# Attention and FFN on one core: TensorE work moved from two tile shapes to 64x32 tiles on two row lanes

## The chip, the cores and the metric

The kernel runs on one core of one Trainium2 chip. The metric is the device time of one execution in microseconds; of several runs the median is given.

## What is computed

`x` has 2048 rows of 640. It is normalised row by row, and two branches read the result: attention with 32 heads of 20 that share one key and one value head, and an FFN with 1728 inner features.

```
xn = layernorm(x)                                  # 2048 x 640
q  = xn @ wq  -> 32 heads of 2048 x 20;  k = xn @ wk;  v = xn @ wv     # one k, one v
p  = softmax(q k^T / sqrt(20));  o = p v           # 32 x 2048 x 2048 scores
out = x + o @ wo + silu(xn @ w1) @ w2
```

Everything is bf16 at the edges, and sums are fp32 in PSUM.

## The kernel before

**Blocks.** The scores are cut into 2048 blocks. A block is one head, 128 keys and 512 queries (one of four chunks of queries); it fills one PSUM bank with keys on the partitions. Four heads make a group. A head sits on 32 partitions (a slot) of `qT` and `kT`: 20 rows of data, two rows for an offset, the rest zero.

**Scores (L1133).** A visit takes up to four blocks, each of another head, on the four row tiles of 32 rows by 128 columns. All blocks of a visit run side by side, one pass of 512 columns.

**Exponentials.** A block's exponentials come from ScalarE (L1156, an exp over one, two or three banks that lie next to each other, into `E`) or from VectorE (L1173). VectorE takes the score, offset by 16045 through the two extra rows, as the bits of a bf16 number; two copies with the phase shifted (L1201 on VectorE or L1207 on GpSimd, three blocks at once) are averaged with it, which gives such a block three PV products in place of one. Only these blocks carry the offset: `kT` is held twice, without it for ScalarE and with it for VectorE.

**PV (L1047).** For a group of four heads, values times exponentials are summed in bank 7 (`UBANK`), each head on its own column tile of 128 rows by 32 columns. A set is one product for each of the four heads. When a group is complete, `end_group` copies the sums out (L1251), a DMA transposes them, and they are divided by their sum.

**Projections (L533, `cols`).** Jobs for q, for the FFN's inner layer (`h`) and for the output (`F`) run as steps of four matmuls, also 128x32, with 512 or 320 columns, and sum in one of the other seven banks.

**Order.** `Sched` is a planner that runs while the program is built: it keeps a clock for each engine, and a price and readiness time for each operation; its result is a fixed order on each queue with semaphores. TensorE's own order is written out by hand from the 64th block on: `ORDER` holds a letter for each step, P for a PV set, J for a projection step, and other letters for score visits, with how many blocks a visit has and how many of them go to VectorE in `VISITS`. `follow` reads it. Ahead of it the start-up (loads, normalisation, keys, values, the first queries) is planned without a list, and behind it `tail` ends the last groups.

**Keys (L1889 to L1906).** `k_job` projects keys; VectorE copies them from PSUM (L1901) and GpSimd makes the second copy with the offset (L1903).

Of the kernel before, what the change touches and what calls it, by code (L numbers as in the profile page):

```python
# [39 lines left out]
OFF_LO = 45.0  # L40
PH = ((0, 1.0), (43, 0.8046875), (86, 0.625))
# [37 lines left out]
RANK = "UofFhqG"  # L79
YIELD = 0.65  # L80
VISITS = {"a": (3, 0), "b": (3, 1), "c": (3, 2), "e": (4, 1), "f": (4, 2), "g": (2, 0), "h": (2, 1), "k": (1, 0), "m": (1, 1), "d": (4, 3)}
ORDER = (
    "BBPPPHMPPGePPPFPPPbJJJJJeMJJJJJPbPPPBfPPMbPBPPPEPPPckPPPHBJJJBJJPBmPPbhhPPBPJGPJJFJPJBGJJJPJJFPPPPgP"
    "PHHPPhgJPPcJKHPhGPPCkJJgHPPPJHbPPPbPPbJJBJPCJJBPPPAPPJbJPJhGJPPdPJgPPPbPPbJJbPJBJJBPJGJJfPJJPbPPBPPP"
    "FPPBPPBJJJJJfGPPPJJJCJJPBgPJPPJBJJJBJJJJJbPPbPPPFPPbPPbPPfJJJJJBGPPJPJJFPJPJPbhJJJJJBGPPPPPfPPbJJJBJ"
    "JbPJJJbPJJBPJJbPJJbJJJbPJJbPPFPPPBPPfPPBJJJJJbPPbJJJJBPPJbJJBJJPPbPPfPPBPPPEPJJJBJJBJPPbJJPbJJJbJPJb"
    "JJJJbPJJbPPFPPBPPBPPEPJPJJbJJJJPbJJBPPJJbPJJJbPPfPPbPPbPPbPPEJJJJBPJPBJPBJJJJbJPJbJJJbJJJJbPPePPPPFP"
    "PBPPFPPaPJJJBJJJJPbJJJBJJJJbPPePPPHhPPPFPPBJJJBJJbJJPJBJJJaPPJJJbJJJJJbPPbPPfPPPBPePPPPFPPPBPPPEJPJJ"
    "JJHbJJJPJBJJJBJPJbPPFPPbPPEPJJJbJJPBJPBJPJJJFgPPPPPPbPPfJJJJJbhJJJJJPePPPPPBcJJJJJBHJJJJJPePPPPBPPfP"
    "PBJJbJJJbPJJPBJJJbPPbJJJJJBJJhJJJePPPPbPPfPPBJJJJJbbPPPPPPFPPBJJJbJJbPPBJJbJJJbPPPPePPBJPJJfJJPJJJgb"  # L90
    "JPPPJPfPPBPPBJJBJJJPbPPPBPPBJJJJBJJJJBJJJbJJJJbJJJJbPFPPPPFPbPPPBPPfPPaPJJBJJPJEPPPBPPPFPPbJJJJJBJJb"
    "JJJPBJPJBJPJbPJJBJJJBPPEPPPPFPPPbPJJbJJJBPJJbJPPbJPJbPJJBJJJbPJJbPJJBPPePPPbPPBJPJPfJPgJJPfPPBPPBJJJ"
    "JBJJJBJJJJBPPBJPJBPJJBJJPBJJPbPPEPPbJJPJJJJEJPJPJJhBPPJBPJJJBJJJBPJJbPPfPPBPPPePPPPFPPbPJJBJJbPJbPPP"
    "fPPBJJPJBJJBJJJJJJeJJJPJJbJJJbPPePPPPPDgPPPbPPPBJJPBJPJBJJJBJPPBJPbPJJbPJJBPJJbJJJJbPPFPPBPPEPJJJJJb"
    "JJJBPJJbJPJbJJJBPPPBJJJJbPPePPPPfPPbPPPbPPfPPbJJJJJbBPPPJJJBJJPJbJJJJPbbPPPJJBJJJPbPbPJJJbJJBPPPPfPP"
    "PbJJBJJJPePPPPBPBJPPJfJJPJPbHJJJJJPfJJJJJPeJJJJJPBbPPPPJbPJBJJbPJbPPBPPfPPbJJJbJJbJJPJbJPJbJJPJbJJPB"
    "PPFPPBJJJJJbbPPPJJPBJJJBPPPbPPPBPPePJJJbJJBPPBPPfPPPbJJJBJJJJbJJJbPJJBPJPbPJBJPPbJJJJbPPFPPAPPPFPPJJ"
    "JBJJPBJJJbJJJJbJJJbJJJJBPPePPBJJPJeJJPPBPPbPPPfPPbPPPFPPbPPBPPEPJJJJJBJJJJBPJJJBJJJBJJJJbPPfPPBPPPeP"
    "JJJJJBJJPBPPbJJPBJJPBPJJJBJJJBPJJbPPfPPPBPPEPPPPFPPbJJJBJPJbPbPPPFPPBJJJJbJJPJJJJfgJJJJJJJJbPJPBPPfP"
    "PBPPBPPFPPbJPJJBPPBJPJBJJJbJPJBPJJBPJJbJJPbPPbJJPJBPPEPJPJPBJJJBPJJBPJJBJPJbPJJBJPJbJPJBJPJbPPfPPBPP"  # L100
    "PePJJJJJBJJJbJJJJbPJJBJJJJBJPbPPPFPPbPPBPPePPJJBJJJPePJJJJhJPePPPPbPPPFPPBJJJJJBbPPPJJJcJJPBgPJJJJJM"
    "ePPPPPPBPfPPJJBJPbPJJbJJhJJJPeJJJJJhBJPJJJJBPPPPfPPBJJJJJbBPPPPPPfPPbJJJbJJbPJPJbJPCJJPgBPJJPJJJbPPP"
    "bPPBJPJBJJJBJPJBJPJBJJJJBJJJBJJPBPPJbPPfPPBPPPePJJJJJbJJJbJJJJbJJJBJJJJbPPfPPAPPPfPPPPFPPBPJJJBJJbJJ"
    "JJJaJJPJJJbJJJJbPPEPPPPfPPPPfPPBPPbPPfPPBJJJJBJJPBJJJbJJPBJJPbPPBJJJJbJPJBPPEPJPJJJBJJJBPPbPJJBJPPBJ"
    "JJBJJJJbJJPBPPFPPBPPaPPPFPPPbPPFPPBJJJJBJPJBJJPbJPPJbJbPPJJJeJJJJJPbPPfPPbPPPFPPAPPBJJJJJJFJJJJGJJJE"
    "JJJJJJbPPFPPbPPFPPBPPEPPbJJJPJJEPPPJJBJJJbPJJBJPPbPPbJPJbJJbJJPbPPFPPbPPbPPBFPBPPBPPbPPFPPBPPAPPBfBP"
    "PBPEPPPFPbPbPPEPPBPPPkbPJJJJJJBJJPbPPEPPA"
# [44 lines left out]
class Op:  # L152
    __slots__ = ("eng", "dur", "fn", "deps", "prio", "seq", "end", "avail", "idx", "inc", "inc_no", "sem",
                 "on_sched", "name", "dma", "mode", "start", "mm", "work", "then", "lock", "rep", "tile", "kt", "w", "x", "na", "at")
# [24 lines left out]


LAT = {"pe": 0.215, "act": 0.27, "dve": 0.14, "pool": 0.19, "sp": 0.0}
# [4 lines left out]
class Sched:  # L186
    def __init__(self, nc, stack):
# [11 lines left out]
        self.held = {}  # L199
        self.lock_end = {"dve": 0.0, "pool": 0.0}  # L200
# [45 lines left out]
    def ready(self, op, extra=0.0):  # L246
        r = op.at
        for d in op.deps:
            if d.avail is None:
                return INF  # L250
            if d.eng == op.eng and not d.dma:
                if op.eng == "pe" or op.eng == "sp":
                    a = d.end
                else:
                    a = d.avail - OWN[op.eng]
# [14 lines left out]

    def commit(self, op, start):
        e = op.eng
        op.start = start
# [8 lines left out]
        op.idx = len(self.order[e])  # L282
# [56 lines left out]
    def emit(self):  # L339
# [3 lines left out]
        every = sorted((op for e in self.engs for op in self.order[e]), key=lambda op: (op.start, op.end, op.idx))  # L343
        for op in every:
            e = op.eng
            mine = seen[e]
            need = {}
            for d in op.deps:
                if d.rep is not None:
                    d = d.rep  # L350
                if not d.dma and d.eng == e and e in ("pe", "sp"):
# [17 lines left out]
        sems = {e: self.sem("done_" + e) for e in self.engs}  # L369
        for e in self.engs:  # L370
            n = 0
            for op in self.order[e]:
                if op.inc and not op.dma:
                    n += 1
                    op.inc_no = n
        out = {e: [] for e in self.engs}
        for e in self.engs:
            for op, w in per[e]:
                def fn(eng, op=op, w=w, e=e):
# [8 lines left out]
                    elif op.inc:  # L388
                        ins.then_inc(sems[e], 1)
# [32 lines left out]
class Job:  # L422
    def __init__(self, name, mms, reads, consume, gate=None, min_step=-1, banks=None, on_start=None, width=0, hold=None, use=None, n=1, mode="M"):
# [14 lines left out]
        self.last = False  # L438
        self.spot = 0


class Builder:
# [17 lines left out]
    def alloc(self):  # L460
# [41 lines left out]
        self.offk = sb([P, 1], F32)  # L502
# [28 lines left out]
    def cols(self, pe, b, n, w, x, start, stop):  # L531
        for j in range(0, w.shape[-1], SLOT):
            ins = pe.matmul(self.bk(b, 0, n, j, j + SLOT), w[:, j:j + SLOT], x, start=start, stop=stop,  # L533
                            tile_position=(0, j), skip_group_check=True)
# [5 lines left out]
    def steps_init(self):  # L540
# [23 lines left out]
        self.pv_started = False  # L564
        self.tq = [[[] for _ in range(4)] for _ in range(self.NG)]
# [101 lines left out]
    def s_reads(self, bs, dv):  # L667
        k = []
        for i, (g, kt, j) in enumerate(bs):
            c, h = g // 8, 4 * (g % 8) + j  # L670
            k += [("kT1" if i in dv else "kT", kt // 2), ("kT", kt // 2), ("qb", c % 2, h)] + self.qkeys(c, h)
# [63 lines left out]
    def step(self, now):  # L735
# [3 lines left out]
        if 0 <= self.at < len(ORDER):  # L739
            return self.follow(ORDER[self.at], now)  # L740
        if self.b_next >= NB:
            return self.tail(now)
# [89 lines left out]
    def follow(self, tok, now):  # L832
        nxt = INF
        if tok == "P":
            n, _, nxt = self.pv_ready(now)
            if n:
                self.do_pv(now, T_PE + self.switch("PV"))
                self.at += 1
                self.stall = 0
                return True  # L840
            if self.debt:
                self.debt -= 1
                self.at += 1
                self.stall = 0
                return self.step(now)
            for d in self.sc.deps_of((), [("UB",)]):
                if d.avail is not None and d.avail > now:
                    nxt = min(nxt, d.avail)
        elif tok == "J":
            job = self.cur_job  # L850
            r = now
            if job is not None and job.step_reads and job.last and self.reads_ready(job.step_reads[0]) > now + 1e-9:
                self.at += 1
                return self.step(now)
            if job is None:
                self.more_jobs()
                r = self.job_ready(self.misc[0]) if self.misc else INF
            if r <= now + 1e-9:
                if job is None:
                    job = self.misc.popleft()  # L860
                    job.bank = self.bank_for_job(job)[1]
                    self.cur_job = job
                    if job.hold is not None:
                        self.heldb[job.hold] = job.bank
                self.do_mm(job, now, job.mms[0][0] + self.switch(job.mode))
                self.at += 1
                self.stall = 0
                return True
            nxt = r
        else:  # L870
            n, nd = VISITS[tok.lower()]
            bt = self.bank_times()
            r = max(self.reads_ready(self.s_reads(self.blocks(n), range(n) if nd else ())), bt[n - 1][0])
            if not self.room(n - nd, nd):
                full, some, _ = self.pv_ready(now)
                if full or some and self.stall > 8:
                    self.do_pv(now, T_PE + self.switch("PV"))
                    self.debt += 1
                    return True
# [1122 lines left out]
```

## Time and profile before

| | |
|---|---|
| three runs | 680.76, 682.35 and 683.6 us; median 682.35 |
| the profiled execution, first to last instruction | 681.4 us |
| granted TensorE clock in it, mean | 0.997 |
| matmuls | 9690 |
| instructions on VectorE, ScalarE, GpSimd | 1103, 765, 455 |

The profiled execution has no time of its own beside its span; the span lies 0.95 us under the median of the runs and inside their range. Views of the trace name engines PE (TensorE's matmuls), PEld (its weight loads), DVE (VectorE), ACT (ScalarE) and POOL (GpSimd). A row of the groups holds the line, the engine, the operation, its tiles and shapes and the count, then behind bars the busy time, the mean of one in ns, and the idle time ahead of them with what ended it. A row of the timeline begins with its start and length, with neighbours of one kind merged. The end of a matmul is modelled in the trace, its start is not.

### The profile page before, as it was taken

Reading aid. Unit: us, or ns where it says so; the run is one execution under the profiler, and the core shown is the slowest. Engines: PE = TensorE matmul, PEld = TensorE weight load, DVE = VectorE, ACT = ScalarE, POOL = GpSimd, SP = SyncE. Lnnn points to the kernel's source line nnn. Section 1 sums busy time; section 2 is a strip of 40 time slices with the busy share of each in tenths; the row PEclk is TensorE's granted clock in tenths of the full one; section 3 lists DMA queues with packets and bytes.
Section 4 is the critical chain, followed back from the end, with each engine's and each line's share of the span. In section 5 each row is a group of like instructions: output and inputs, shape, how many; then the busy total and the mean of one; then the engine's idle time right before and its main releaser. Section 6 shows DMA issues by size and latency. Waiting matters only on the chain.

```text
span 681.4 us, 22653 instructions
## 1 busy us (share of the span) xinstructions
PE 669.8 (98%) x9690; PEld 230.8 (34%) x9690; DVE 623.7 (92%) x1103; ACT 661.3 (97%) x765; POOL 563.9 (83%) x455
## 2 busy tenths in 40 slices
PE   9899999999999999999999999999999999999997
PEld 4333323333333333333333333333333333333323
DVE  7879999999899999999999999999989999999996
ACT  6989999999999999999999999999999999999995
POOL 5559888888888998887888899788899898878873
PEclk9989999999999999999999999999999999999999
DMA  7457301000103000011012000001011100000002
GB/s 207 88 203 234 116 18 14 6 14 18 17 17 55 11 9 19 23 23 37 19 29 61 10 17 23 24 17 32 15 29 48 29 10 12 11 19 20 20 17 64
DMA packets 53241, 28.18 MB, mean 41 GB/s; under 512 B 39094, under 2 KB 52502, under 8 KB 53142
## 3 DMA queue, kind: packets, MB, share of 16 engines
q1 hardware_dynamic: 52854, 26.40, 15.2%
q8 instruction: 78, 1.28, 0.8%
q10 hardware_dynamic: 288, 0.33, 0.1%
q14 instruction: 21, 0.17, 0.1%
HBM read 11.44 MB, written 2.62 MB: 21 GB/s over the span
## 4 chain that ended last, share of the span: by engine, by line
PE 81%; ACT 10%; DVE 7%; DMA 1%; issue 1%; ACTq 0%
PE psall L1047 28%; PE psall L1133 25%; PE psall L533 25%; ACT sbt L1156 10%; DVE sbt L1173 3%; PE psall L967 1%; DMA sbt<-sbt 1%; DVE sbt L1722 1%; DVE sbt L1201 1%; DVE sbt L1403 1%; PE psall L1893 1%; PE psall L954 0%; DVE sbt L1885 0%; DVE sbt L1251 0%; PE psall L1297 0%
## 5 line engine op out<-in xcount | busy, mean ns | idle before, releaser
L1156 ACT ACTIVATE sbt<-psall 128x1024 bf16<-128x1024 f32 (+2 forms) x680 | 626.5, 1056 | 5.5 <-PE psall L1133 4.9
L1207 POOL TENSOR_TENSOR sbt<-sbt 128x768 int32<-128x768 int32 (+2 forms) x378 | 526.2, 1418 | 87.0 <-DVE sbt L1201 74.6
L1173 DVE TENSOR_SCALAR sbt<-psall 128x512 int16<-128x512 f32 x711 | 466.1, 684 | 41.2 <-PE psall L1133 32.7
L1047 PE MATMUL psall<-sbt 128*32 128x512 bf16 x3470 | 281.3, 385 | 0.3 <-DVE sbt L1901 0.2
L1133 PE MATMUL psall<-sbt 32*128 32x512 bf16 x2048 | 251.4, 384 | 2.4 <-ACT sbt L1156 1.0
L533 PE MATMUL psall<-sbt 128*32 128x320 bf16 (+1 forms) x3863 | 235.1, 331 | 0.3 <-DVE sbt L1173 0.3
L1133 PEld LDWEIGHTS psall<-sbt 32*128 32x128 bf16 x2048 | 66.4, 91 | 235.9 <-issue 87.7
L533 PEld LDWEIGHTS psall<-sbt 128*32 128x32 bf16 x3863 | 87.0, 95 | 86.5 <-issue 43.0
L1047 PEld LDWEIGHTS psall<-sbt 128*32 128x32 bf16 x3470 | 70.8, 95 | 102.4 <-issue 71.0
L1201 DVE TENSOR_SCALAR sbt<-sbt 128x1536 int16<-128x1536 int16 (+1 forms) x114 | 65.9, 583 | 0.6
L1403 DVE SCALAR_TENSOR_TENSOR sbt<-sbt,psall 128x512 bf16<-128x512 bf16 (+1 forms) x56 | 37.9, 677 | 0.1
L1395 ACT ACTIVATE sbt<-psall 128x512 bf16<-128x512 f32 x54 | 33.9, 627 | 0.9 <-PE psall L533 0.4
L1239 POOL TENSOR_TENSOR sbt<-sbt 128x320 bf16<-128x320 bf16 x31 | 22.6, 729 | 5.4 <-DVE sbt L1201 5.4
L1251 DVE CAST sbt<-psall 128x512 bf16<-128x512 f32 x31 | 21.2, 684 | 1.2 <-PE psall L1047 1.0
L967 PE MATMUL psall<-sbt 128*128 128x512 bf16 (+3 forms) x66 | 18.0, 403 | 1.6 <-DVE sbt L1656 1.2
L1501 DVE SCALAR_TENSOR_TENSOR sbt<-psall,sbt 128x320 bf16<-128x320 f32 x28 | 13.4, 487 | 1.3 <-PE psall L533 0.9
L1352 DVE TENSOR_SCALAR sbt<-psall 128x512 bf16<-128x512 f32 (+1 forms) x19 | 13.0, 684 | 0.9 <-PE psall L533 0.7
L1722 DVE BATCH_NORM_STATS2 sbt<-sbt 128x6 f32<-128x320 bf16 x24 | 10.4, 468 | 2.6 <-DMA sbt<-in_A_x_dram 2.6
L1903 POOL TENSOR_SCALAR sbt<-sbt 128x256 bf16<-128x256 bf16 x8 | 3.8, 479 | 9.8 <-DVE sbt L1752 5.7
L1748 POOL TENSOR_SCALAR sbt<-sbt 128x640 bf16<-128x640 bf16 x7 | 6.1, 877 | 5.0 <-DVE sbt L1790 3.7
L967 PEld LDWEIGHTS psall<-sbt 128*128 128x128 bf16 x66 | 6.1, 105 | 10.3 <-issue 4.0
L1893 PE MATMUL psall<-sbt 128*128 128x256 bf16 x40 | 5.9, 274 | 3.3 <-DVE sbt L1924 1.4
(80 smaller groups left out, 90.1 us busy)
## 6 DMA issues: line engine op xcount, KB each, us to landing
sbt<-in_A_x_dram SPq DMA_DIRECT2D x31, 160.0 KB, 3.4
out_dram<-sbt SPq DMA_DIRECT2D x15, 160.0 KB, 1.8
sbt<-in_B_w_dram SPq DMA_DIRECT2D x5, 432.0 KB, 5.4
sbt<-sbt SPq DMA_DIRECT2D x105, 20.0 KB
sbt<-in_B_w_dram SPq DMA_DIRECT2D x13, 160.0 KB, 3.0
sbt<-sbt SPq DMA_DIRECT2D x1, 1024.0 KB, 6.5
sbt<-sbt SPq DMA_TRANSPOSE x58, 2.5
sbt<-in_A_wo_dram SPq DMA_DIRECT2D x5, 160.0 KB, 2.8
```

What stands on the lines that cost most here:

```text
L533: ins = pe.matmul(self.bk(b, 0, n, j, j + SLOT), w[:, j:j + SLOT], x, start=start, stop=stop, tile_position=(0, j), skip_group_check=True)
L967: return pe.matmul(self.bk(b, 0, n), self.zero[:, 0:P], self.zero[:, 0:n], start=True, stop=True)
L1047: ins = pe.matmul(self.bk(UBANK, 0, QW, r, r + SLOT), self.v[:, it.w, it.kt, :], it.x(), start=f, stop=False, tile_position=(0, r), skip_g ...
L1133: ins = pe.matmul(self.bk(bank[i]), self.kT[r:r + SLOT, 1 if i in dv else 0, kt * P:(kt + 1) * P], self.qT[r:r + SLOT, g % 8, (g // 8) % 2 ...
L1156: return a.activation(self.E[:, (b0 + lo) * QW:(b0 + lo + m) * QW], self.ps[:, b * BANK:(b + m) * BANK], AF.Exp, scale=ACT_SCALE)
L1173: return v.tensor_scalar(self.Z[:, zs, zp * QW:(zp + 1) * QW], self.bk(bb), 0.0, ZMAX, ALU.max, ALU.min)
L1201: sc.new("dve", td, lambda v, k=k: v.tensor_scalar(self.Y[:, zs, k, 0:w], self.Z[:, zs, 0:w], float(PH[k + 1][0]), None, ALU.add), zk, yk, ...
L1207: sc.new("pool", tp, lambda v, k=k, cb=cb: v.tensor_tensor(self.Y[:, zs, k, 0:w].bitcast(I32), self.Z[:, zs, 0:w].bitcast(I32), cb, ALU.ad ...
L1239: op = sc.new(eng, 0.75 if eng == "pool" else t_dve_ps(16 * DH), lambda v: v.tensor_tensor(dst, ut[:, :, :, 0:DH], rb, ALU.mult), [key, (" ...
L1251: ev = sc.new("dve", t_dve_ps(QW), lambda v: v.tensor_copy(self.U[:, up, :], self.bk(UBANK)), [("UB",)], [("U", up)], prio=U_PRIO, name=f" ...
L1395: sc.new("act", t_act(QW), lambda a: a.activation(t, src, AF.Tanh, scale=0.5), [("B", b)], [("tb", tp)], prio=X_PRIO, name=f"th{c}_{fk}")
L1403: sc.new("dve", t_dve_ps(QW), lambda v, r0=r0, r1=r1, ht=ht: v.scalar_tensor_tensor(out=ht[r0:r1, :], in0=t[r0:r1, :], scalar=1.0, in1=src ...
```

## The change

From the 64th block on no TensorE work uses the two old shapes. The array is cut into two row lanes, rows 0 to 63 and 64 to 127, with four column tiles of 32 each; every step is four matmuls on one lane.

- A score block is one lane's step. It takes 64 rows, that is two heads' slots, and `kT` now holds two copies that each keep only the even or only the odd slots (`kmask`), so the other head adds nothing. Its four matmuls make 32 keys each. Heads 0 and 1 of a group use lane 0, heads 2 and 3 lane 1.
- A PV set and a projection step are done twice, once on each lane with half of the contraction, and both halves sum into the same place in PSUM. The lanes are not on one bank at the same time: a step waits by semaphore for the other lane's last step on that bank (`lane_ready`, with a semaphore for each lane).
- A group's sums are copied out when both lanes have done the last set.
- All blocks carry the offset, so there is one form of key, written by two VectorE instructions with mask and offset; GpSimd's copy goes. ScalarE's exp takes the offset off again by a constant bias.
- The list is written anew: 5588 letters. `a` and `b` are a score for ScalarE on lane 0 and 1, `d` and `e` one for VectorE, `p` and `q` a PV set's half, `j` and `k` a projection step's half. Capital `A` or `B` ends a group of banks that one exp takes: 635 groups of two and two of one. Capital `D` or `E` puts the first shifted copy on VectorE.

| letters, large and small | lane 0 | lane 1 |
|---|---|---|
| scores for ScalarE | 637 | 635 |
| scores for VectorE | 355 | 357 |
| PV | 874 | 874 |
| projections | 928 | 928 |

The list before has 936 J, 869 P and 636 visits with 1981 blocks, 696 of them for VectorE; between visits and the rest it changes 1169 times.

The core of the diff:

```diff
+ACT_BIAS = -ACT_SCALE * (OFF_HI + OFF_LO)
+T_ISSUE = 0.028
+T_DRAIN = 0.1
+DEPTH = 4
+HOLD = 0.02
+PE = ("pe", "p0", "p1")
...
-    def cols(self, pe, b, n, w, x, start, stop):
+    def cols(self, pe, b, n, w, x, start, stop, lane=None):
+        lo, hi = (0, P) if lane is None else (64 * lane, 64 * lane + 64)
         for j in range(0, w.shape[-1], SLOT):
-            ins = pe.matmul(self.bk(b, 0, n, j, j + SLOT), w[:, j:j + SLOT], x, start=start, stop=stop,
-                            tile_position=(0, j), skip_group_check=True)
+            ins = pe.matmul(self.bk(b, 0, n, j, j + SLOT), w[lo:hi, j:j + SLOT], x[lo:hi, :], start=start, stop=stop,
+                            tile_position=(lo, j), skip_group_check=True)
...
+    def lane_ready(self, deps, lane):
+        r = 0.0
+        for d in deps:
+            if d.rep is not None:
+                d = d.rep
+            if d.avail is None:
+                return INF
+            if d.eng != PE[1 + lane] or d.dma:
+                r = max(r, d.avail)
+        return r
...
+    def lane_score(self, tok, lane, now):
...
+        def fn(pe):
+            r = 64 * lane
+            for c in range(0, P, SLOT):
+                ins = pe.matmul(self.bk(b, 0, QW, c, c + SLOT), self.kT[r:r + 64, j % 2, kt * P + c:kt * P + c + SLOT],
+                                self.qT[r:r + 64, g % 8, (g // 8) % 2, :], start=True, stop=True, tile_position=(r, c),
+                                skip_group_check=True)
+            return ins
...
+        def efn(a):
+            return a.activation(self.E[:, b0 * QW:(b0 + n) * QW], self.ps[:, b1 * BANK:(b1 + n) * BANK], AF.Exp,
+                                scale=ACT_SCALE, bias=ACT_BIAS)
...
+    def lane_pv(self, lane, now):
...
+        def fn(pe):
+            lo = 64 * lane
+            for it, f in zip(items, first):
+                r = it.tile * SLOT
+                ins = pe.matmul(self.bk(UBANK, 0, QW, r, r + SLOT), self.v[lo:lo + 64, it.w, it.kt, :], it.x()[lo:lo + 64, :],
+                                start=f, stop=False, tile_position=(lo, r), skip_group_check=True)
+            return ins
...
+        if new["last"] and min(self.sp) == n + 1:
+            self.u_open = False
+            self.begun = [False] * 4
+            self.cg += 1
+            self.end_group(g)
...
-                dst = self.kT[:, 0, j * 256:j * 256 + 256]
-                d1 = self.kT[:, 1, j * 256:j * 256 + 256]
-                sc.new("dve", t_dve_ps(256), lambda v: v.tensor_copy(dst, src), [("B", b)], [("kT", j)], prio=0.4,
-                       name=f"kev{j}")
-                sc.new("pool", 0.46, lambda g: g.tensor_scalar(d1, dst, self.offk[:, :], 1.0, ALU.add,
-                                                                      ALU.mult), [("kT", j), ("offk",)],
-                       [("kT1", j)], prio=1.0, name=f"k1_{j}").lock = True
+                for p in range(2):
+                    sc.new("dve", t_dve_ps(256), lambda v, p=p: v.tensor_scalar(
+                        self.kT[:, p, j * 256:j * 256 + 256], src, self.kmask[:, p:p + 1], self.offk[:, p:p + 1],
+                        ALU.mult, ALU.add), [("B", b), ("offk",), ("kmask",)], [("kT", j, p)], prio=0.4, name=f"kev{j}")
```

More of the change, by code (lines that the diff above doesn't have):

```diff
@@ L342, in emit @@
         known = {}
[L343 removed]
+        every = sorted((op for e in self.engs for op in self.order[e]), key=lambda op: (op.issue, op.end, op.idx))
         for op in every:
[L345 removed]
+            e = "pe" if op.eng in PE else op.eng
             mine = seen[e]
@@ L1529, in out_job @@
         job.last = lastk or dst == "open"
+        job.lanes = not job.last and dst != "yx"
         job.spot = FIN.index((i, e))
```

513 lines of the change are left out of this document (382 added, 131 removed).

## The prediction

> **What bounds the kernel now.** I read the page first, for the shares of the engines and the chain.
>
> ```profile
> span 681.4 us, 22653 instructions
> PE 669.8 (98%) x9690; PEld 230.8 (34%) x9690; DVE 623.7 (92%) x1103; ACT 661.3 (97%) x765; POOL 563.9 (83%) x455
> PE 81%; ACT 10%; DVE 7%; DMA 1%; issue 1%; ACTq 0%
> ```
>
> Two engines are above 97% and the chain runs through PE for four fifths of its length. So the next question is how much of PE's and ACT's time is work. The change begins behind the 64th score block. That block starts at 45.4 us and the last one at 669.8 us, which cuts the span into three stretches, and the windows view gives each of them.
>
> ```profile
> 0.00:45.40 45.40, 40.10 (x358) 17.26 (x358) 34.33 (x107) 35.55 (x49) 24.30 (x51) 0.96 0.67 184
> 45.40:669.80 624.40, 621.76 (x9161) 208.61 (x9158) 583.81 (x983) 621.35 (x711) 537.75 (x404) 1.00 0.13 31
> 669.80:681.40 11.60, 7.93 (x179) 4.94 (x175) 5.53 (x15) 4.43 (x7) 1.87 (x2) 0.99 0.17 59
> ```
>
> The columns behind the length are PE, PEld, DVE, ACT and POOL. All that matters lies in the 624.4 us of the middle. To see what a busy PE does there I read its timeline in a quiet place.
>
> ```profile
> 300.10 0.40 PE L1133 MATMUL psall<-sbt 32*128 32x512 bf16 x4
> 300.42 0.83 PE L1047 MATMUL psall<-sbt 128*32 128x512 bf16 x12
> 301.18 0.39 PE L1133 MATMUL psall<-sbt 32*128 32x512 bf16 x3
> 301.50 0.61 PE L1047 MATMUL psall<-sbt 128*32 128x512 bf16 x8
> 302.05 0.39 PE L1133 MATMUL psall<-sbt 32*128 32x512 bf16 x3
> 302.37 0.40 PE L533 MATMUL psall<-sbt 128*32 128x512 bf16 x4
> 302.60 0.39 PE L1047 MATMUL psall<-sbt 128*32 128x512 bf16 x4
> 302.82 0.39 PE L533 MATMUL psall<-sbt 128*32 128x512 bf16 x4
> ...
> 478.11 1.27 PE L533 MATMUL psall<-sbt 128*32 128x320 bf16 x32
> 479.31 0.39 PE L1133 MATMUL psall<-sbt 32*128 32x512 bf16 x3
> ```
>
> Four matmuls make a pass. Passes of one tile shape follow each other every 0.22 us (302.37, 302.60, 302.82). A score pass (32*128) is left after 0.32 us (301.18 to 301.50), and twelve PV matmuls, three passes, after 0.76 us (300.42 to 301.18). With a pass at 0.217 us both leave 0.105 us for a change of tile shape. Eight passes of 320 columns and one change take 1.20 us (478.11 to 479.31), so 0.137 us a pass. Now the counts of the middle stretch:
>
> ```profile
> L1047 PE MATMUL psall<-sbt 128*32 128x512 bf16 x3390 | 273.3, 383 | 0.2
> L533 PE MATMUL psall<-sbt 128*32 128x320 bf16 x2304 | 123.1, 302 | 0.0
> L533 PE MATMUL psall<-sbt 128*32 128x512 bf16 x1395 | 104.1, 382 | 0.3 <-DVE sbt L1173 0.3
> L1385 PE MATMUL psall<-sbt 128*32 128x512 bf16 x40 | 2.7, 381 | 0.0
> ```
>
> The order list has 636 score visits (138.0 us at 0.217). PV makes 848 passes (184.0). Projections make 349 + 10 passes of 512 columns (77.9) and 576 of 320 (78.9). That is 479 us of passes. The list changes between scores and the rest 1169 times: at 0.105 us, 123 us. Together 602 of 624.4 us, so PE is a true bound, with 22 us of other idling. ACT is the second:
>
> ```profile
> 299.70 40.92 ACT L1156 ACTIVATE sbt<-psall 128x1024 bf16<-128x1024 f32 x45
> ...
> L1156 ACT ACTIVATE sbt<-psall 128x1024 bf16<-128x1024 f32 x545 | 520.5, 1072 | 1.8 <-PE psall L1133 1.4
> L1156 ACT ACTIVATE sbt<-psall 128x1536 bf16<-128x1536 f32 x42 | 63.6, 1513 | 0.1
> L1156 ACT ACTIVATE sbt<-psall 128x512 bf16<-128x512 f32 x70 | 40.9, 633 | 0.2 <-PE psall L1133 0.2
> L1395 ACT ACTIVATE sbt<-psall 128x512 bf16<-128x512 f32 x54 | 33.9, 627 | 0.9 <-PE psall L533 0.4
> ```
>
> 45 exps back to back take 40.92 us, 0.909 us each, against 1.072 us for one alone: neighbours overlap by 0.163 us. With this taken off each form, ACT needs 545 x 0.909 + 42 x 1.350 + 70 x 0.470 + 54 x 0.464 = 495.4 + 56.7 + 32.9 + 25.1 = 610 us. It is therefore at 98% too, with about 14 us of idling that its busy figure hides.
>
> **The change part by part.** The new list has 5588 steps, 2794 on each lane. A step is four matmuls of 64x32 on one row lane.
>
> *PE.* The 1169 changes of shape go: -123 us. Scores get dearer: a visit put up to four blocks side by side in one pass, now a block occupies one lane for a pass. Each lane has 992 score steps (215.3 us), 874 PV steps (189.7) and 928 projection steps (359 of 512 columns, 77.9, and 569 of 320, 78.0). That is 561 us for a lane, if the two run side by side, in place of 602: -41 us. Side by side is not shown for 64x32; what bounds it is the row of 300.10, where four row tiles finish in 0.40 us together, and the row of 300.42, where four column tiles do. I take full overlap, as both halves of the shape overlap by themselves; the other end is none, 1122 us.
>
> *Weight loads and issue.* Each lane step issues four loads and four matmuls, so both double.
>
> ```profile
> 300.42 0.34 PEld L1047 LDWEIGHTS psall<-sbt 128*32 128x32 bf16 x12 [0.23 <-issue]
> ```
>
> Here twelve loads are over in 0.34 us, while their twelve matmuls (the row of 300.42) run on for 0.83 us: later passes' weights come in under running matmuls. The issue of four loads and four matmuls fits in a fraction of a pass, so I cost both at nothing; without the cover a step would cost 0.11 us more, four of these loads (0.34 / 3). [...]
>
> *Handing a bank from lane to lane.* This is what the change adds. A sum in PSUM gets the keys 0 to 63 from one lane and 64 to 127 from the other, one after the other, with a semaphore between. In the new list PV changes its lane 328 times; projections change at the same places in the other direction. Behind the waiting PV step stand, on the same queue, the steps of both lanes.
>
> ```profile
> 301.62 0.69 DVE L1173 TENSOR_SCALAR sbt<-psall 128x512 int16<-128x512 f32 x1 [0.23 <-PE psall L1133]
> ```
>
> The pass of 301.18 released this DVE step at 301.62: 0.44 us, of which 0.217 are the pass, so a semaphore costs 0.22 us. The list puts one to three score steps (0.217 us each) on free banks between most lane changes, so I take nothing; the ends are 0 and 0.22 us each, 0 to 72 us.
>
> *ACT.* Exps now come as 635 pairs and 2 singles: 635 x 0.909 + 2 x 0.470 + 25.1 = 603 us, 7 less. The constant bias:
>
> ```profile
> L1710 ACT ACTIVATE sbt<-sbt 128x640 bf16<-128x640 bf16 x4 | 2.9, 734 | 0.1
> L1742 ACT ACTIVATE sbt<-sbt 128x640 bf16<-128x640 bf16 x3 | 2.6, 916 | 0.0
> ```
>
> L1742 takes scale and bias from SBUF, L1710 a number, and 0.182 us separate them, 0.091 for each operand. The new bias is written as a number, so I take 0; as an operand it would be 637 x 0.091 = 58 us.
>
> *DVE and POOL.*
>
> ```profile
> L1173 DVE TENSOR_SCALAR sbt<-psall 128x512 int16<-128x512 f32 x698 | 457.2, 684 | 35.5 <-PE psall L1133 27.1
> L1201 DVE TENSOR_SCALAR sbt<-sbt 128x1536 int16<-128x1536 int16 x103 | 61.2, 598 | 0.5
> L1201 DVE TENSOR_SCALAR sbt<-sbt 128x1024 int16<-128x1024 int16 x6 | 2.7, 444 | 0.0
> ...
> L1207 POOL TENSOR_TENSOR sbt<-sbt 128x768 int32<-128x768 int32 x344 | 496.2, 1467 | 80.5 <-DVE sbt L1201 71.1 <-DVE sbt L1173 8.8
> ```
>
> 712 blocks go to DVE in place of 698 (+14 x 0.655 us) and 127 shifted copies in place of 109 (+18 x 0.594): 583.8 + 9.2 + 10.7 = 604 us. POOL loses some 20 adds of 1.467 us and stays behind. So DVE comes up to ACT.
>
> *Start.* Keys are now written twice by DVE, and POOL's copy goes.
>
> ```profile
> L1901 DVE CAST sbt<-psall 128x256 bf16<-128x256 f32 x8 | 3.3, 417 | 0.3 <-PE psall L1893 0.2
> L1903 POOL TENSOR_SCALAR sbt<-sbt 128x256 bf16<-128x256 bf16 x8 | 3.8, 479 | 9.8 <-DVE sbt L1752 5.7 <-DVE sbt L1901 3.2 <-DVE sbt L1201 0.9
> ```
>
> That adds 8 x 0.417 = 3.3 us to DVE, which idles for 11 of the first 45.4 us; the ends are -0.5 (POOL's wait gone) and 3.3, and I take +0.5, for the one copy ahead of the first scores.
>
> *The sum.* Behind the change the middle stretch has three floors: lanes 561, ACT 603, DVE 604 us. ACT idled for 14 us with PE as its rival; PE lets go of 41 us, but DVE closes in, so I leave ACT 9.5: 612.5. Then 45.9 + 612.5 + 11.6 = 670.0 us, 11.4 less than the execution's 681.4. The runs shown have a median of 682.35, 0.95 above the span, so 671.0.
>
> **The rivals.**
> - **Handing over is exposed (slower).** Each of the 328 lane changes costs the whole 0.22 us on both lanes: 561 + 72 + the 22 of PE's old idling = 655, and 45.9 + 655 + 11.6 + 0.95 = 713.5. It decides from 0.09 us a change, (612.5 - 22 - 561) / 328, and makes the kernel slower than now from 0.13. For it: one queue feeds both lanes, so one late semaphore stops both. Against it: the score steps between. [...]
> - **DVE takes the bound (no change).** DVE had 40.6 us without work in the middle, 27.1 of them waiting for scores. If half stays, 604 + 20 = 624 us and the time stays at 682. For it: the 604; against it: steadier scores.
> - **Loads are not covered.** 2794 x 0.11 = 307 us more on a lane, 868 in all: 926. [...]
> - **The lanes do not run side by side**, so the change doesn't do what it says: 1122 us, 1180.
> - **The bias becomes an operand.** ACT 603 + 58 + 9.5 = 670.5: 729.
>
> **How the numbers follow.** Forecast 0.55, with 659 to 678 as its own range; handing over 0.22, DVE 0.14, loads 0.03, no overlap 0.02, bias 0.04. The range runs from 658 (ACT without idling, 45.9 + 603 + 11.6 + 0.95 = 661.5, less 1 us for the start's lower end and 1.6 by which the fastest run shown, 680.76, lies under the median) to 708, which leaves out the last three rivals and the far end of handing over. Half a per cent, 3.4 us, is about what a measurement of this kernel can tell. Faster 0.57: the forecast and a little of the DVE case; same 0.13; slower 0.30: handing over and the last three, with a little from DVE.
>
> **What would show it.** Right: the number of matmuls more than doubles; two groups of four matmuls run over the same time; ACT's pairs follow every 0.91 to 0.93 us; the middle stretch lies near 612 us. Wrong: weight loads waiting for PE itself 328 times (handing over); DVE busy above 98% with ACT waiting on no one but PE's scores (DVE); exps longer than 1.1 us (bias); steps of one lane further apart than 0.23 us in long runs (loads, overlap).

## The result and the profile after

The changed kernel is slower: a median of 735.98 us over 4 runs (732.15 to 738.42), against 681.79 us for the kernel before in the same session (680.76 to 683.6). The ratio is 1.0787, with a 95% interval of 1.0748 to 1.0826. The forecast was 671.0 with a range of 658 to 708, so the time went the other way. In the profiled execution the span is 736.6 us.

The page of the kernel after, the lines that answer to those of before; the third is a DMA queue, with its packets and MB, that the prediction did not look at:

```profile
span 736.6 us, 49090 instructions
PE 694.4 (94%) x22787; PEld 415.6 (56%) x22790; DVE 645.7 (88%) x1163; ACT 665.2 (90%) x744; POOL 536.0 (73%) x424
q8 instruction: 178, 2.92, 1.7%
PE 82%; DVE 6%; issue 4%; SPq 3%; ACT 2%; DMA 1%; POOL 0%; DVEq 0%; ACTq 0%
```

The same queue on the page of before:

```profile
q8 instruction: 78, 1.28, 0.8%
```

No engine is above 94% any more: the bound has gone from PE and ACT to something that all of them wait for. The program has 49,090 instructions in place of 22,653, and the queue whose kind the page calls "instruction" moves 178 packets in place of 78. The windows of after show where the time went. They are cut as before: at the start of the 64th score block and of the last one.

```profile
0.00:47.10 47.10, 41.15 (x377) 19.07 (x380) 39.46 (x121) 34.96 (x47) 21.42 (x43) 0.96 0.65 177
47.10:722.20 675.10, 641.81 (x22097) 389.65 (x22098) 600.35 (x1027) 627.05 (x691) 513.58 (x382) 0.99 0.14 31
722.20:736.60 14.40, 11.48 (x324) 6.84 (x312) 5.85 (x16) 3.16 (x6) 0.95 (x1) 1.00 0.18 62
```

The middle stretch went from 624.4 to 675.1 us, the start from 45.4 to 47.1, and the tail from 11.6 to 14.4. The waits of after (who waited for whom, us in all, times, longest) say who came late:

```profile
ACT sbt L1060 <- PE psall L1032: 39.9, 66, 3.7
...
PEld psall L1138 <- PE psall L1138: 17.5, 63, 0.8
...
PE psall L594 <- issue: 12.4, 24, 1.1
...
PE psall L1032 <- issue: 7.1, 18, 0.7
```

ScalarE's exp (now L1060) waits 39.9 us for scores (L1032). PE's matmuls in their turn wait for "issue", that is, for nothing that the profile names: before, the 2304 projection matmuls of 320 columns had 0.0 us of any wait. (For weight loads, PEld, such a wait says little: in before the loads for PV have 71.0 us of it, while the PV matmuls have 0.3 us of any idle time ahead of them.) In the chain, issue went from 1% to 4% of the span. Waits of one lane for the other are 17.5 us for PV (the second row) and 6.9 us for the projections. PE's timeline in after shows what such a wait looks like:

```profile
348.22 0.39 PE L1138 MATMUL psall<-sbt 64*32 64x512 bf16 x4
348.35 0.30 PE L594 MATMUL psall<-sbt 64*32 64x320 bf16 x3
349.41 0.31 PE L594 MATMUL psall<-sbt 64*32 64x320 bf16 x1 [0.76 <-issue]
349.42 0.40 PE L1138 MATMUL psall<-sbt 64*32 64x512 bf16 x4
```

A projection step (L594) stops after three of its four matmuls, and the fourth comes a microsecond later. No semaphore stands between the four. The trace's records give a pattern. Count TensorE's instructions, loads, matmuls and the few semaphore instructions together, from the first record on, and take each start that comes more than 0.24 us after the one before it: 85 of these stops stand at one and the same place in a block of 256 instructions (the 191st), 56.7 us together, and no other place has more than 3. So they lie a multiple of 256 instructions apart, and each ends 1.1 to 1.6 us (median 1.4) after a packet of queue 8 landed. The page's counts agree: 22,787 matmuls and 22,790 loads are 178.0 times 256, and there are 178 packets; in the kernel before, 2 x 9690 is 75.7 times 256, and there are 78. The 56.7 us are about as much as the 54.2 us by which the kernel got slower.

**Theory:** TensorE's instructions come in blocks of 256 at a limited rate. A lane step issues eight instructions where half a pass issued four, and the stream can't keep up. **Rivals:** handing banks from lane to lane is exposed; weight loads aren't covered; the constant bias costs ScalarE time; the lanes don't run side by side.

### The profile page after: what moved, and what is told of

Its sections match the earlier page's. It is cut to its first block, busy times and chain, and to the rows that moved or that the text cites. A ratio compares the mean times of both kernels' runs of the same rounds, so it can differ in the third digit from the quotient of the medians.

```text
span 736.6 us, 49090 instructions
## 1 busy us (share of the span) xinstructions
PE 694.4 (94%) x22787; PEld 415.6 (56%) x22790; DVE 645.7 (88%) x1163; ACT 665.2 (90%) x744; POOL 536.0 (73%) x424
## 4 chain that ended last, share of the span: by engine, by line
PE 82%; DVE 6%; issue 4%; SPq 3%; ACT 2%; DMA 1%; POOL 0%; DVEq 0%; ACTq 0%
PE psall L1032 31%; PE psall L1138 27%; PE psall L594 21%; DVE sbt L1076 4%; PE psall L1266 1%; SPq L1947 1%; DMA sbt<-sbt 1%; ACT sbt L1457 1%; SPq L1845 1%; ACT sbt L1060 1%; DVE sbt L2211 1%; SPq L1663 1%; PE psall L1346 1%; DVE sbt L1502 0%; DVE sbt L1474 0%
## 5 line engine op out<-in xcount | busy, mean ns | idle before, releaser
L1060 ACT ACTIVATE sbt<-psall 128x1024 bf16<-128x1024 f32 x637 | 608.3, 1034 | 48.2 <-PE psall L1032 39.9
L1508 POOL TENSOR_TENSOR sbt<-sbt 128x768 int32<-128x768 int32 (+1 forms) x355 | 502.0, 1439 | 159.3 <-DVE sbt L1502 146.2
L1138 PE MATMUL psall<-sbt 64*32 64x512 bf16 x6876 | 525.1, 379 | 6.0 <-issue 4.6
L1032 PE MATMUL psall<-sbt 64*32 64x512 bf16 x7936 | 490.5, 379 | 14.3 <-issue 7.1
L594 PE MATMUL psall<-sbt 64*32 64x320 bf16 (+3 forms) x7530 | 460.4, 328 | 13.1 <-issue 12.4
L594 PEld LDWEIGHTS psall<-sbt 64*32 64x32 bf16 (+1 forms) x7530 | 191.7, 92 | 88.8 <-issue 25.3
L1032 PEld LDWEIGHTS psall<-sbt 64*32 64x32 bf16 x7936 | 166.5, 90 | 118.8 <-DVE sbt L1076 39.6
L1138 PEld LDWEIGHTS psall<-sbt 64*32 64x32 bf16 x6876 | 178.8, 91 | 81.1 <-issue 19.2
L1502 DVE TENSOR_SCALAR sbt<-sbt 128x1536 int16<-128x1536 int16 (+2 forms) x145 | 75.7, 540 | 0.2
L1457 ACT ACTIVATE sbt<-psall 128x1024 bf16<-128x1024 f32 (+2 forms) x22 | 23.2, 1123 | 5.3 <-PE psall L1434 3.9
L1266 PE MATMUL psall<-sbt 128*128 128x512 bf16 (+6 forms) x59 | 16.9, 425 | 2.5 <-DVE sbt L1982 1.2
L1535 DVE RECIPROCAL sbt<-sbt 128x16 f32<-128x16 bf16 x31 | 7.6, 245 | 5.3 <-DMA sbt<-sbt 5.3
```

The lines of the kernel that those rows point to most:

```text
L594: ins = pe.matmul(self.bk(b, 0, n, j, j + SLOT), w[lo:hi, j:j + SLOT], x[lo:hi, :], start=start, stop=stop, tile_position=(lo, j), skip_gr ...
L1032: ins = pe.matmul(self.bk(b, 0, QW, c, c + SLOT), self.kT[r:r + 64, j % 2, kt * P + c:kt * P + c + SLOT], self.qT[r:r + 64, g % 8, (g // 8 ...
L1060: return a.activation(self.E[:, b0 * QW:(b0 + n) * QW], self.ps[:, b1 * BANK:(b1 + n) * BANK], AF.Exp, scale=ACT_SCALE, bias=ACT_BIAS)
L1138: ins = pe.matmul(self.bk(UBANK, 0, QW, r, r + SLOT), self.v[lo:lo + 64, it.w, it.kt, :], it.x()[lo:lo + 64, :], start=f, stop=False, tile ...
L1266: return pe.matmul(self.bk(b, 0, n), self.zero[:, 0:P], self.zero[:, 0:n], start=True, stop=True)
L1457: return a.activation(self.E[:, (b0 + lo) * QW:(b0 + lo + m) * QW], self.ps[:, b * BANK:(b + m) * BANK], AF.Exp, scale=ACT_SCALE, bias=ACT ...
```

## The experiments

### Half of the score matmuls

```diff
-            for c in range(0, P, SLOT):
+            for c in range(0, 64, SLOT):
                 ins = pe.matmul(self.bk(b, 0, QW, c, c + SLOT), self.kT[r:r + 64, j % 2, kt * P + c:kt * P + c + SLOT],
                                 self.qT[r:r + 64, g % 8, (g // 8) % 2, :], start=True, stop=True, tile_position=(r, c),
                                 skip_group_check=True)
```

> Leaves out two of the four matmuls of each score step on the lanes (64 of 128 keys); a step still occupies its lane for 512 columns, and all waits, lane changes and other work stay. Theory A (TensorE's instruction stream is the bound: blocks of 256 instructions arrive no faster than one per some 3.5 us, 73 a us): 7936 of 45600 instructions go, a block then lasts over 4 us, the gaps at block borders mostly go; 36 to 40 us less than the changed kernel, so 695 to 702 us. Theory B (handing a bank from lane to lane): nothing changes, 730 to 738 us. Theory C (weight loads not covered): a step loses half its loads, 64 x 32 by four becomes two, some 10 to 30 us less.

It took 686.32 us, 1.0081 times before (1.0053 to 1.011), less than any of the three theories gave. The profiled execution is the quickest of five (680.88 us), so its waits are rather low. Page, and ScalarE's pairs in the groups by shape:

```profile
PE 667.3 (98%) x18819; PEld 405.4 (60%) x18822; DVE 639.0 (94%) x1163; ACT 653.0 (96%) x744; POOL 535.1 (79%) x424
q8 instruction: 147, 2.41, 1.5%
```

```profile
L1060 ACT ACTIVATE sbt<-psall 128x1024 bf16<-128x1024 f32 x635 | 596.2, 1051 | 3.4 <-PE psall L1032 2.4 <-issue 0.2 <-PE psall L1138 0.2
```

The two matmuls left in a score step still have 512 columns each, so by my estimate the step still takes a pass (four side by side on one lane take 0.217 us, L59 below, where a single one takes 0.376), and every semaphore is still there. Yet 49.7 us of the 54.2 are gone, and ScalarE's wait for scores falls from 39.9 to 2.4 us. The waits of lane for lane hardly move:

```profile
PEld psall L1138 <- PE psall L1138: 13.7, 51, 0.6
```

The stops at one place of the block fall from 85 to 7 (2.8 us). So handing over is not what cost the 54 us.

### Half of the projections too, and half of the projections alone

```diff
-        for j in range(0, w.shape[-1], SLOT):
+        for j in range(0, w.shape[-1] if lane is None or full else 64, SLOT):
             ins = pe.matmul(self.bk(b, 0, n, j, j + SLOT), w[lo:hi, j:j + SLOT], x[lo:hi, :], start=start, stop=stop,
                             tile_position=(lo, j), skip_group_check=True)
```

(`full` is set for the q projections, which stay whole. The first of the two runs has this edit and the one above, the second has this one alone.)

> As the run before, and two of the four matmuls of each step of the FFN and output projections on the lanes are left out as well (q projections stay whole). Steps, waits and lane changes stay. Theory A: the stream falls to some 31000 instructions, 5.7 us a block, so no gap at block borders is left; 680 to 695 us, little under the run before, and what still lies over the forecast of 671 us is not the stream's. Theory B: 730 to 738 us. Theory C: another 10 to 30 us under the run before.

> The changed kernel without two of the four matmuls of each step of the FFN and output projections on the lanes; scores are whole, all steps, waits and lane changes stay. Theory A: 6600 of 45600 instructions go, 39000 are left, somewhat more than with half the scores (37700, 686 us): 686 to 697 us. If the gain of the run with half the scores came from the scores themselves (their writes to PSUM, their loads): 725 to 738 us.

Both: 682.49 us, ratio 1.0 (0.9986 to 1.0015). Projections alone: 683.26 us, 1.0013 (1.0 to 1.0027), with all scores whole; 686 to 697 was expected. Two edits in different work, which save 7,936 and 6,621 instructions, give nearly the same back, 49.7 and 52.7 us, and both together only 53.5. That is how a limit behaves that no longer binds once the load is some 15% lower. Both edits also leave out matmuls, so they don't yet say whether it is the instructions or the matmuls that count. Windows of the run with both, cut at blocks 64, 200 and the last:

```profile
46.70:94.10 47.40, 43.97 (x941) 23.20 (x932) 41.24 (x71) 42.66 (x50) 37.40 (x27) 0.96 0.47 132
94.10:665.80 571.70, 570.06 (x13901) 342.53 (x13903) 551.13 (x955) 570.20 (x642) 474.43 (x353) 1.00 0.12 23
665.80:680.10 14.30, 11.46 (x292) 7.15 (x282) 6.61 (x17) 3.62 (x7) 1.51 (x2) 1.00 0.21 69
```

The same cuts in the kernel before:

```profile
45.40:88.30 42.90, 41.69 (x527) 13.49 (x523) 40.99 (x73) 42.09 (x59) 35.91 (x27) 1.00 0.47 143
88.30:669.80 581.50, 580.08 (x8638) 195.11 (x8635) 542.83 (x911) 579.26 (x653) 501.83 (x378) 1.00 0.10 22
```

From block 200 on, the thinned lanes need 571.7 us where before needed 581.5. There a gain of 9.8 us is left, with half of the matmuls gone, but the stretch ahead of block 200 gives back 4.5 us, the tail 2.7 and the start (46.7 against 45.4) 1.3.

### The same work, with the instructions put back

This is the direct test: the projections stay halved, and each matmul left out is made up for by weight loads alone.

```diff
         for j in range(0, w.shape[-1] if lane is None or full else 64, SLOT):
+            if lane is not None and not full:
+                for _ in range(2):
+                    pe.ldweights(w[lo:hi, j:j + SLOT], tile_position=(lo, j))
             ins = pe.matmul(self.bk(b, 0, n, j, j + SLOT), w[lo:hi, j:j + SLOT], x[lo:hi, :], start=start, stop=stop,
                             tile_position=(lo, j), skip_group_check=True)
```

> The kernel after in which each FFN and output projection step on a lane leaves out two of its four matmuls with their loads (as in the run that halved these steps alone, 683.3 us), but four more weight loads of the same weights stand in their place, two ahead of each matmul that is left. So the number of TensorE instructions is that of the kernel after (about 49,100 in all, 178 fetches of instructions), while the matmuls stay those of the halved run (about 19,480). Sums of these steps are not the reference's. Theory (the instruction stream, 256 instructions in no less than about 3.5 us, sets the end): the loss comes back, 728 to 740 us. Rival (what the halved run saved was the array's work or its matmuls, not their instructions; loads run beside matmuls at no cost): 683 to 688 us. In between would mean that both count.

It took 729.17 us (724.77 to 731.79), ratio 1.0704 (1.0651 to 1.0757): 45.9 of the 52.7 us come back.

```profile
span 726.0 us, 49090 instructions
PE 692.2 (95%) x19475; PEld 445.6 (61%) x26102; DVE 644.3 (89%) x1163; ACT 666.0 (92%) x744; POOL 535.8 (74%) x424
q8 instruction: 178, 2.92, 1.6%
```

The matmuls are those of the halved run, the instructions and the 178 packets those of after. Bare loads could also have a price of their own, so it matters where the time goes. It goes to the block borders: 80 stops are back at the same place in a block of 256, 48.0 us together, where the halved run has no place with more than 4. So the number of instructions sets most of the loss, and the matmuls at most the 6.8 us that didn't come back.

### TensorE alone: the price of each thing

A kernel with no other engine's work runs each kind of step some hundred times (one run, 471.37 us). (It leaves out the whole of the reference's computation and copies x to the output.) Its core:

```python
def lane_320(pe, p):
    for l in range(2):
        lo = 64 * l
        for j in range(0, 128, 32):
            pe.matmul(bank(4 * l + p % 4, 320, j, j + 32), W[lo:lo + 64, j:j + 32], X[lo:lo + 64, 0:320], start=True,
                      stop=True, tile_position=(lo, j), skip_group_check=True)
```

> TensorE alone, nothing waits, the output is a copy of x: passes of four 128x32 matmuls of 512 columns with 0, 1 and 3 additional weight loads for each matmul; steps on one 64x32 lane; on both lanes with 512 and with 320 columns; then changes of shape, 128x32 against 64x32 and 64x128 against 64x32. Theory A: 0.217 us a pass with 0 and 1 loads (37 and 55 instructions a us), 20 instructions / 73 = 0.27 us with 3; one lane 0.217; a pair on both lanes 0.217 to 0.225 with 512 columns (74 a us), and 16 / 73 = 0.22 in place of 0.137 us with 320 columns. Theory B: 0.217 and 0.137 us on both lanes, since no bank is handed over. Theory C: 0.33 us on one lane. A change of shape that drains adds 0.105 us each way: 0.64 us for a 128x32 pass and a lane pair, or a 64x128 pair and a lane pair; 0.43 us if it doesn't.

Its timeline; L40 are passes of 128x32, L47 the same with one load more for each matmul, L54 with three more, L59 one lane of 64x32, L66 two lanes, L73 two lanes with 320 columns:

```profile
18.59 54.13 PE L40 MATMUL ps<-x,w 128*32 128x512 bf16 x1000
72.55 43.33 PE L47 MATMUL ps<-x,w 128*32 128x512 bf16 x800
...
120.98 3.01 PE L54 MATMUL ps<-x,w 128*32 128x512 bf16 x51 [0.35 <-issue]
124.42 3.03 PE L54 MATMUL ps<-x,w 128*32 128x512 bf16 x51 [0.42 <-issue]
...
148.34 53.71 PE L59 MATMUL ps<-x,w 64*32 64x512 bf16 x992
...
202.12 55.79 PE L66 MATMUL ps<-x,w 64*32 64x512 bf16 x1975
...
261.72 2.37 PE L73 MATMUL ps<-x,w 64*32 64x320 bf16 x128 [0.88 <-issue]
265.18 2.37 PE L73 MATMUL ps<-x,w 64*32 64x320 bf16 x128 [1.09 <-issue]
...
312.15 1.92 PE L73 MATMUL ps<-x,w 64*32 64x320 bf16 x97 [1.10 <-issue]
314.01 0.40 PE L24 MATMUL ps<-x,w 128*32 128x512 bf16 x4
314.34 0.41 PE L30 MATMUL ps<-x,w 64*32 64x512 bf16 x8
314.68 0.40 PE L24 MATMUL ps<-x,w 128*32 128x512 bf16 x4
```

The rows of L73 show the limit by itself. No semaphore, no other engine, and yet PE works in bursts of exactly 128 matmuls: with their loads, 256 instructions. From 261.72 to 312.15 there are 14 bursts, 3.60 us each on average, 3.46 for the first of them (261.72 to 265.18): **71 instructions a microsecond**. L54, with five instructions for each matmul, stops every 51 matmuls, again 255 instructions (124.42 - 120.98 = 3.44 us). In the rows that keep below this rate nothing stops: L40 and L59 issue 8 instructions in 0.217 us (37 a microsecond), L47 12 (55). L66 needs 16 in 0.217 us, 74 a microsecond, and sits on the edge at 0.224 for a pair of steps (55.79 / 1975 x 8, less the last one's tail). Two lanes do run side by side (0.224 us a pair against 0.217 for one lane's step), and a load more for each matmul costs nothing (L47: 43.33 / 200 = 0.217 us a pass). A pair of 320 columns takes 0.225 us where before a whole pass took 0.137; inside a burst it takes 0.13 ((2.37 - 0.30) / 16, 0.30 being one matmul), so the array could do it.

The last three rows are a change of shape: 0.335 us from one shape to the next, 0.118 over the pass. Between 64x128 and 64x32, where only the columns change, it is 0.32 to 0.34 us too. L59 keeps 0.217 us a step on one lane, with four loads and four matmuls on the same 64 rows in each, where 0.33 was expected of loads that aren't covered.

### The bias

```diff
-                                    AF.Exp, scale=ACT_SCALE)
+                                    AF.Exp, scale=ACT_SCALE, bias=ACT_BIAS)
```

In the kernel before, with the offset in all keys. The first run also took GpSimd's second copy of the keys away:

> The kernel before with one part of the change alone: one form of key with the offset, written by one VectorE instruction, and the constant bias in the exp; GpSimd's copy of the keys goes; tile shapes and order list stay. If the bias and the keys cost nothing, as forecast: exps of 1024 columns stay at 1.07 us, and the time stays within 679 to 685 us. If the bias costs an operand's 0.091 us: 58 us more, 740 us, which would explain the whole loss.

724.96 us, ratio 1.0637 (1.0613 to 1.0662), but this says nothing of the bias: without the copy the planned start ends earlier (42.7 in place of 45.4 us), and the hand-written list then met other blocks than it was written for. ScalarE's exps of two banks took 1.039 us on average, not longer than the 1.072 of before. The second run keeps the copy, and so the plan:

> The kernel before with the keys' offset in the one copy that all scores read, written by VectorE from PSUM, and the constant bias in the exp; GpSimd still writes its (now unread) copy, so that every queue keeps its order and its waits. If bias and keys cost nothing: within 0.5% of the kernel before, exps of 1024 columns near 1.07 us, and the 42 us that the run with one form of key lost come from the order list, which there met other blocks than it was written for. If they cost: 720 us and more.

682.34 us, ratio 1.0001 (0.9986 to 1.0017), and exps of two banks take 1.072 us as before. A bias written as a number costs nothing.

### More loads in the kernel before

```diff
+            for _ in range(MORE):
+                pe.ldweights(w[:, j:j + SLOT], tile_position=(0, j))
             ins = pe.matmul(self.bk(b, 0, n, j, j + SLOT), w[:, j:j + SLOT], x, start=start, stop=stop,
```

(MORE is 3, in scores and PV as well, so that the stream is about as long as in after.)

> The kernel before with three additional weight loads ahead of each matmul of the scores, PV and projections on 128x32 and 32x128 tiles: 9400 matmuls get 28000 more instructions, no array time, no waits; TensorE's stream grows from 19900 to 48000 instructions, a little more than the changed kernel's 45600. Theory A (256 instructions in no less than about 3.6 us, 71 a us): 47000 / 71 = 662 us for the middle stretch in place of 624, with gaps that carry no wait: 725 to 750 us. If only row lanes and their handing over are slow: 680 to 690 us.

810.23 us, ratio 1.1878 (1.1843 to 1.1912), more than either theory gave. Its timeline:

```profile
301.45 0.41 PE L1140 MATMUL psall<-sbt 32*128 32x512 bf16 x4
301.84 0.63 PE L1052 MATMUL psall<-sbt 128*32 128x512 bf16 x8
302.52 0.40 PE L1140 MATMUL psall<-sbt 32*128 32x512 bf16 x3
```

None of these rows begins with a stop, but a score pass is left after 0.39 us where before had 0.32, and two PV passes after 0.68 in place of 0.55 (the rows 301.50 and 302.05 of before). So loads that cost nothing between passes of one shape (L47) cost 0.07 and 0.13 us at these changes of shape: some 0.2 us there and back, so by estimate 117 us for 1169 changes if all are like these two, of the 128 us lost. Elsewhere in this run 26 stops stand at one place of a block of 256, 17.9 us together. The run therefore confounds two costs and does not isolate the stream; the refilled run above does, as its lanes don't change shape.

### Handing a bank over, by itself

```python
def hand_2(pe, l, sem, wait):
    lo = 64 * l
    if wait[1] > 0:
        pe.wait_ge(wait[0], wait[1])
    for j in range(0, 128, 32):
        ins = pe.matmul(bank(7, 512, j, j + 32), W[lo:lo + 64, j:j + 32], X[lo:lo + 64, :], start=True, stop=True,
                        tile_position=(lo, j), skip_group_check=True)
    ins.then_inc(sem, 1)
```

(`wait` is the other lane's semaphore at its last count; all turns sum into bank 7.)

> TensorE alone, the output is a copy of x. Both lanes write one bank in turn, each waiting for the other by semaphore, with no step between, with one step on the lane that waits, and with three steps between (one there, one on each lane on other banks). Handing over costs what a semaphore costs: 0.217 + 0.22 = 0.44 us a turn with nothing between; with one step between 0.44 too, with the step hidden in it; with three steps (two on the waiting lane, 0.43) 0.43 to 0.65 us. Last, 128x32 passes with two no-operations ahead of each matmul, 16 instructions a pass: if any instruction counts, 0.217 to 0.23 us a pass, at the edge of 16 / 71; more if a no-operation has a price of its own.

(277.34 us in all, one run, TensorE alone.) With nothing between, the first turns come every 0.469 us, as the loads of three of them show:

```profile
23.11 0.10 PEld L38 LDWEIGHTS ps<-x,w 64*32 64x32 bf16 x4 [0.57 <-PE ps L38]
23.58 0.10 PEld L38 LDWEIGHTS ps<-x,w 64*32 64x32 bf16 x4 [0.37 <-PE ps L38]
24.05 0.10 PEld L38 LDWEIGHTS ps<-x,w 64*32 64x32 bf16 x4 [0.37 <-PE ps L38]
```

From 28 us on, and in the whole part with one step between, they come every 0.687 us, where 0.44 was expected; the granted clock is 0.53 on average from 22.70 to 102.00 us and 0.50 from 103.00 to 182.00, so this is no price at full speed. The timeline of the part with three other steps (L69) between two turns (L56):

```profile
210.31 0.40 PE L56 MATMUL ps<-x,w 64*32 64x512 bf16 x4
210.32 0.61 PE L69 MATMUL ps<-x,w 64*32 64x512 bf16 x12
210.77 0.40 PE L56 MATMUL ps<-x,w 64*32 64x512 bf16 x4
210.79 0.61 PE L69 MATMUL ps<-x,w 64*32 64x512 bf16 x12
```

Turns follow every 0.467 us, as with nothing between: a step of 0.217 and 0.25 for the semaphore, in which the other steps run. The forecast's 0.22 us from a row of VectorE was near, and so was its cover. A part with idle instructions between the matmuls told nothing: the trace shows none of them, and the run's 34 packets of queue 8 are no more than its 8,880 loads and matmuls fill.

## Why the prediction was wrong

**The step that failed** is "Weight loads and issue", and in it "The issue of four loads and four matmuls fits in a fraction of a pass, so I cost both at nothing". The loads were rightly costed at nothing (L59: 0.217 us a step with four of them). The issue was not: I priced the issue of one step by itself and never the stream of all steps. 5588 steps of 8 instructions are 44,704, or 174.6 blocks of 256; at the 3.60 us measured by itself, 629 us (at 3.46, its first interval, 604). That is a fourth floor of the middle stretch, above the 561 of the lanes, the 603 and 604 of ACT and DVE, and at 3.60 us above the 612.5 of the sum; with it alone the forecast would have been slower than before. The stretch took 675.1. The other 46 us fit a stream that can't make up for what it loses: steps of 320 columns ask for 16 instructions in 0.137 us, 117 a microsecond, where 71 come, and while PE waits for a bank the stream gains nothing that the traces show: counted from the first instruction of a block (the 191st of 256 in both kernels), the next packet lands after 2.2 us (median) in after, and after 2.6 us in before too, where a block lasts 8.4 us. Of the 173 blocks that end in after's middle stretch, 84 end in a stop and last 3.79 us on average; the other 89 last 4.04. How the 46 us split between blocks that come late and time not made up is argued, not measured. None of the rivals had this cause; the handing rival gave 713.5 with the right sign for a wrong reason.

**Shape changes.** Right: they are gone, and a change is worth what the sum had (0.118 by itself against 0.105).

**Lanes side by side.** Right for 512 columns (0.224 us a pair). For 320 columns the array would do it (0.13 us a pair inside a burst), but the stream doesn't let it (0.225).

**Handing over at nothing.** Nearly right. PE's waits of lane for lane, PV and projections together, are 24.4 us in after and 18.2 with half of the scores, a run that is within 1.1% of before.

**ACT, the bias, DVE.** Right: no cost in the run with the bias; exps of two banks took 1.036 us, not over 1.1. VectorE never became the bound.

**The sum without the stream.** The run with both halvings shows it best, with the reserve that it has less work in the array too: a span of 680.1 against the 670.0 of the sum. From block 200 on it needs 571.7, where the sum, spread evenly, has 581.5 x 612.5 / 624.4 = 570.4: 1.3 us off. Blocks 64 to 200 take 47.4 in place of 42.1 (+5.3), the tail 14.3 in place of 11.6 (+2.7), and the start 46.7 in place of 45.9 (+0.8). So even where the stream's stops are gone this version only draws level. (Two slips in the working change nothing: the range's lower end adds up to 658.9, not 658, and inside the list of before there are 1168 changes of shape, not 1169.)

What is late between blocks 64 and 200 stands in SyncE's timeline. After:

```profile
76.92 5.38 SPq L1663 DMA_DIRECT2D sbt<-sbt  x7
82.34 1.63 SPq L1521 DMA_TRANSPOSE sbt<-sbt  x1
```

Before:

```profile
71.69 5.23 SPq L1361 DMA_DIRECT2D sbt<-sbt  x7
76.96 1.26 SPq L1220 DMA_TRANSPOSE sbt<-sbt  x1
```

And VectorE's timeline of after:

```profile
80.91 0.54 DVE L1502 TENSOR_SCALAR sbt<-sbt 128x1536 int16<-128x1536 int16 x1
85.18 0.25 DVE L1535 RECIPROCAL sbt<-sbt 128x16 f32<-128x16 bf16 x1 [3.73 <-DMA sbt<-sbt]
```

The transposition of the second group's sums is issued 5.4 us later than before (82.34 for 76.96). The same seven issues stand ahead of it on the queue in both kernels, but they start 5.2 us later. VectorE, whose order the kernel fixes, stands 3.73 us at the reciprocal for it (0.49 before) with score conversions behind. In the run with both halvings, where no place of the block has more than 3 stops, that wait is 3.52 us, so it doesn't come from the stream; there the transposition is issued only 2.1 us later than before (79.03), so the late issue isn't all of it. TensorE's granted clock is lower behind this wait (0.50 from 85.20 to 90.00 us in after, windows view): over blocks 64 to 200 it is 0.93 in after and 0.96 with both halvings, against 1.00 in before.

```profile
47.10:97.50 50.40, 46.37 (x1344) 24.23 (x1342) 42.12 (x73) 43.45 (x50) 37.91 (x28) 0.93 0.42 126
```

That is worth at most 0.07 x 50.40 = 3.5 us in after and 0.04 x 47.40 = 1.9 of the 5.3 us. All this was read from the traces; no run moved that DMA. The tail's 2.7 us weren't taken apart either.

## What to carry to other kernels

Before cutting TensorE work into smaller tiles, count its instructions, loads and matmuls, for each microsecond that the plan gives them, and compare this with the rate at which the stream arrives (here 256 in 3.4 to 4.0 us, 3.6 on average). The sign of the limit is a matmul that waits for "issue" in the middle of a step with no semaphore near, stops that lie a multiple of one instruction count apart (here 256), and a growing count on the instruction queue of the page. To test for it, take matmuls away and put bare loads in their place: if the time returns, it was the instructions.

## What was not expected of the hardware

- TensorE's instructions arrive in blocks of 256 (85 stops of after at one place of 256, bursts of 256 with TensorE alone). With TensorE alone, blocks that had to be waited for began 3.44 to 4.04 us apart, 3.60 on average in a row of 14. Above that rate, 71 instructions a microsecond, PE stopped: a pair of 320 columns took 0.225 us where it took 0.13 inside a burst.
- Loads that cost nothing under matmuls of the same shape (L40 and L47 of the kernel with TensorE alone: 0.217 us a pass without and with one more) cost 0.07 us (score to PV) and 0.13 us (PV to score) across a change of shape in the kernel before, with three more for each matmul.
- In the handing kernel, PE's granted clock fell to a mean of 0.53 while turns came with nothing between them (the windows view, columns PE, PEld, POOL, clock, DMA share, GB/s):

```profile
22.70:102.00 79.30, 70.87 (x487) 12.66 (x475) 0.00 (x0) 0.53 0.00 1
```

Nothing but the waits for the other lane's semaphore stood between them. In the changed kernel the clock stayed at 0.99 in the middle, so its part in the 54 us is at most the 3.5 us named above.
